# Attention with a mixture step: a new order of the first 12 blocks with K turned ahead of x, and a new end

## The chip, the cores and the metric

The kernel runs on one core of one Trainium2 chip. The core has five engines that run side by side: TensorE (matrix products; PE in the profile, its weight loads PEld), VectorE (DVE), ScalarE (ACT), GpSimd (POOL) and SyncE (SP), which here only issues DMAs. Each engine carries out its own list of instructions strictly in order and waits on semaphores for the others. The metric is the time of one execution on the device in microseconds (us), the median of several runs; lower is better.

## What is computed

The reference, cut to what matters (B=1, S=2048, D=640; 32 heads of width 192, a window of the last 512 keys):

```python
xn = layernorm(x)
q  = (xn @ wq).reshape(heads)                 # 2048 x 32 x 192
p  = softmax(q @ k[-512:].T * 192 ** -0.5)    # per head, 2048 x 512
s  = concat_heads(p @ v[-512:]) @ wo          # 2048 x 640
B  = xn, with an FFN result added to the 2 rows that score highest
out = x + s * silu(B)
```

All inputs and the output are bf16; sums are kept in fp32.

## The kernel before

The 32 heads are 8 groups of 4 (`GROUP`), a group is two head pairs, and the 2048 rows are 4 tiles of 512. A **step** is one group, one tile of 512 rows and one head pair (64 steps); it makes q for its pair, transposed, in three column sets c = 0, 1, 2 (`qT`, written by `q_whole` or the two-phase `q_phase`). A step is two **blocks** of 256 rows, 128 blocks in all, and a block has two halves a = 0, 1 of 128 rows. For a block b and half a:

- `S.b.a` (`scores`, line 367): six products of q and K into one of two score buffers in PSUM (`ps_s`, two buffers), 128 rows by 2 heads by 512 keys.
- `M.b.a` (`row_max`, line 372): VectorE takes the negated row maxima.
- `E.b.a` (`exps`, line 377): ScalarE takes the exponentials, one operation per head, and thereby empties the score buffer. Behind them SP issues a DMA that transposes the result into `pT`: one per half where b stands in `SPLIT`, otherwise one for the whole block.
- `P.b` (`o_item`): 32 products with V (line 406, `o_ps`), whose extra column is the row sum; VectorE takes its reciprocal, and VectorE (`v`) or ScalarE (`a`) scales each head's half into `o_sb`; SP issues the DMA that transposes it into `oT`.
- `W.k` (`w_item`, line 447): 24 products of `oT` with wo for two tiles of 128 rows and one half of the 640 output columns. In the first group they are copied into `s_acc`; in later groups they are added to it; in the last group each is multiplied by the gate, which lies in `xn` by then (line 473), and added to `s_acc`, which holds `s*g + x` by then (line 475 or 478), and stored (476, 479).

In the main loop (line 952) every block has the same fixed order (`BLOCK`). The head, blocks 0 to 11, and the end, blocks 126 and 127, follow two lists written out by hand, `FIRST` (line 602) and `LAST` (line 998). `first` and `last` turn each token into instructions; an engine gets its instructions in the order of the tokens. So the lists set, for each engine and for SP's DMA queue, who stands behind whom.

In the head the kernel also loads x, K, V, wq and wo; normalizes x (`st`, `nw`, `ap`, or `sa` for statistics on ScalarE; GpSimd takes some of the scalings, `ap.n.g`); transposes each normalized row tile on TensorE (`turn.n`, line 282, copied out by ScalarE or VectorE, line 283); turns the first K the same way (`kturn`, line 276) and later ones by DMA after a reordering on GpSimd (`ko`, `kT`); and doubles wo on GpSimd into the other 64 partitions (`wd`, line 151). q, P and W results and the turned tiles share four PSUM banks in turn (`f_tile`) until line 949, where they become one pair for q and two single banks for P and W.

In the end P of block 126 and 127 can't wait for DMA transposes, so the exponentials of block 127 (`U`, line 389) and the results of 126 and 127 (`T`, line 433) are turned on TensorE. W.124 to W.127 store each half of the columns by itself; the sums of W.124 and W.125 are GpSimd's, those of W.126 and W.127 VectorE's.

## Time and profile before

| | |
|---|---|
| median of 3 runs | 792.52 us (791.92 to 792.92) |
| profiled execution, its own time | 793.03 us |
| its span, first to last instruction | 791.3 us |
| TensorE busy | 777.6 us (98%) |
| VectorE, ScalarE, GpSimd busy | 579.0, 527.9, 338.8 us |
| mean granted TensorE clock | 0.998 |

The profile is of one execution. A row of the timeline gives the start in us from the span's beginning, the duration, the engine, the line of the kernel, the operation, what it writes and reads, and how many were merged; in square brackets stands how long the engine was idle before it and who ended that. A row of the groups gives the busy time of all of a kind, the mean of one in ns, and the idle time before them. The ends of matrix products are modelled, and one may overlap the next by about a tenth of a microsecond.

### The profile page before, as it was taken

How to read it: one execution, taken by the hardware profiler on the slowest of the kernel's cores; microseconds unless marked ns; L12 is line 12 of the kernel's file. 1: busy time of each engine (PE TensorE's matmuls, PEld its weight loads, DVE VectorE, ACT ScalarE, POOL GpSimd, SP SyncE). 2: the span in 40 equal slices, each digit the busy share in tenths (PEclk: the TensorE clock that was granted, in tenths of full speed). 3: DMA queues.
4: the chain of work that ended last, by engine and by line, in shares of the span. 5: the costliest groups of instructions: out<-in, count | busy, mean ns of one | idle time of the engine just before them, and what ended most of it. 6: DMA issues, size and time to landing. Idle time of an engine off the chain costs nothing.

```text
span 791.3 us, 26980 instructions
## 1 busy us (share of the span) xinstructions
PE 777.6 (98%) x11356; PEld 571.5 (72%) x11356; DVE 579.0 (73%) x1069; ACT 527.9 (67%) x954; POOL 338.8 (43%) x280
## 2 busy tenths in 40 slices
PE   8899999999999999999999999999999999999997
PEld 4457677777777777777777777777777777777775
DVE  7898788877777776767776766766766766776775
ACT  5676666667666677767666666766666666666662
POOL 1334110023110226626120101569977795256895
PEclk9999999999999999999999999999999999999999
DMA  9989999899999999999999999999999999999992
GB/s 231 199 175 170 175 190 167 141 189 164 174 193 186 179 200 199 184 174 195 179 195 198 190 206 191 159 190 188 159 171 185 148 180 183 185 171 167 187 186 84
DMA packets 447130, 142.18 MB, mean 180 GB/s; under 512 B 414180, under 2 KB 446438, under 8 KB 447008
## 3 DMA queue, kind: packets, MB, share of 16 engines
q1 hardware_dynamic: 437312, 130.88, 99.7%
q10 hardware_dynamic: 8672, 6.72, 3.3%
q0 software_dynamic: 1024, 2.85, 1.3%
q8 instruction: 89, 1.46, 0.8%
q14 instruction: 33, 0.27, 0.1%
HBM read 40.31 MB, written 2.63 MB: 54 GB/s over the span
## 4 chain that ended last, share of the span: by engine, by line
PE 89%; DMA 4%; DVE 3%; ACT 2%; issue 1%; SPq 0%; DVEq 0%; ACTq 0%
PE w L447 24%; PE q_ps L340 23%; PE o_ps L406 20%; PE s L367 19%; DMA oT<-o_sb 2%; DVE nm L372 2%; ACT pexp L377 1%; PE q_ps L309 1%; DMA x_in<-in_A_x_dram 1%; DMA pT<-pexp 1%; DMA v_sb<-in_A_v_cache_dram 1%; DMA xsT<-xsel 0%; DVE fin_o L475 0%; PE tp L282 0%; PE gu_ps L787 0%
## 5 line engine op out<-in xcount | busy, mean ns | idle before, releaser
L372 DVE TENSOR_REDUCE nm<-s 128x2 f32<-128x1024 f32 x256 | 312.9, 1223 | 137.8 <-PE s L367 136.1
L377 ACT ACTIVATE pexp<-s,nm 128x512 bf16<-128x512 f32 x512 | 324.1, 688 | 95.3 <-DVE nm L372 91.0
L340 PE MATMUL q_ps<-xnT,wq_g 64*128 64x512 bf16 (+1 forms) x2340 | 232.4, 323 | 0.0
L447 PE MATMUL w<-wo_g,oT 64*128 64x320 bf16 x3072 | 231.5, 296 | 0.2
L367 PE MATMUL s<-kT,qT 64*128 64x512 bf16 x1536 | 211.4, 376 | 2.5 <-ACT pexp L377 1.7
L447 PEld LDWEIGHTS <-oT 64*128 64x128 bf16 x3072 | 169.1, 94 | 59.7 <-DMA oT<-o_sb 1.4
L406 PEld LDWEIGHTS <-pT 64*128 64x128 bf16 x4096 | 177.3, 94 | 31.4 <-issue 2.8
L406 PE MATMUL o_ps<-v_sb,pT 64*128 64x193 bf16 x4096 | 195.3, 243 | 2.9 <-DMA pT<-pexp 1.8
L420 ACT ACTIVATE o_sb<-o_ps,rl 128x192 bf16<-128x192 f32 x250 | 91.6, 418 | 133.6 <-DVE rl L413 128.3
L340 PEld LDWEIGHTS <-wq_g 64*128 64x128 bf16 x2340 | 125.5, 99 | 46.1 <-DVE qT L313 0.5
L151 POOL COPY wo_g<-wo_g 64x1920 bf16<-64x1920 bf16 x32 | 57.4, 1797 | 189.4 <-DMA wo_g<-in_A_wo_dram 188.5
L367 PEld LDWEIGHTS <-qT 64*128 64x128 bf16 x1536 | 84.5, 94 | 57.6 <-DVE qT L313 3.0
L470 DVE TENSOR_TENSOR s_acc<-s_acc,w 128x320 f32<-128x320 f32 x192 | 84.9, 484 | 31.8 <-PE w L447 31.7
L352 ACT ACTIVATE qT<-q_ps 128x1024 bf16<-128x1024 f32 x114 | 92.4, 811 | 7.4 <-PE q_ps L340 1.4
L417 DVE TENSOR_TENSOR o_sb<-o_ps,rl 128x384 bf16<-128x384 f32 x131 | 73.0, 557 | 4.5
L121 POOL COPY k_perm<-k_raw 128x768 bf16<-128x768 bf16 x30 | 24.2, 827 | 95.4 <-DMA k_raw<-in_A_k_cache_dram 68.7
L877 POOL TENSOR_SCALAR yh<-y_bc,oh 128x640 f32<-128x640 f32 x32 | 60.3, 1886 | 5.4 <-DMA y_bc<-y_d 2.6
L878 POOL TENSOR_TENSOR xn<-xn,yh 128x640 bf16<-128x640 bf16 x32 | 45.0, 1406 | 2.7
L864 POOL TENSOR_TENSOR tz<-tz,xn 128x640 f32<-128x640 f32 x16 | 22.4, 1400 | 54.2 <-ACT tz L863 54.2
L413 DVE RECIPROCAL rl<-o_ps 128x2 f32<-128x2 f32 x256 | 30.5, 160 | 12.2 <-PE o_ps L406 7.6
L937 POOL TENSOR_TENSOR s_acc<-s_acc,x_fin 128x640 f32<-128x640 f32 x16 | 22.4, 1400 | 11.0 <-DMA x_fin<-in_A_x_dram 10.1
L865 POOL TENSOR_TENSOR xn<-tz,xn 128x640 bf16<-128x640 f32 x16 | 22.4, 1398 | 1.3
(138 smaller groups left out, 275.9 us busy)
## 6 DMA issues: line engine op xcount, KB each, us to landing
wo_g<-in_A_wo_dram SPq DMA_DIRECT2D x32, 240.0 KB, 4.2
k_raw<-in_A_k_cache_dram SPq DMA_DIRECT2D x32, 192.0 KB, 3.3
v_sb<-in_A_v_cache_dram SPq DMA_DIRECT2D x32, 192.0 KB, 4.1
wq_g<-in_A_wq_dram SPq DMA_DIRECT2D x14, 288.0 KB, 3.7
pT<-pexp SPq DMA_TRANSPOSE x246, 4.2
wq_g<-in_A_wq_dram SPq DMA_DIRECT2D x14, 192.0 KB, 3.1
x_fin<-in_A_x_dram SPq DMA_DIRECT2D x16, 160.0 KB, 3.8
oT<-o_sb SPq DMA_TRANSPOSE x126, 3.6
```

Of the source, the lines that this page charges most:

```text
L151: nc.gpsimd.tensor_copy(out=grp[g][("wo", pr)][half(1), cs, :], in_=grp[g][("wo", pr)][half(0), cs, :])
L340: mm = nc.tensor.matmul(q_ps[k][:, 0:n] if type(q_ps) is list else q_ps[:, k, 0:n], lhsT=wq[half(r), dc, c:2 * Dh:3], rhs=xnT[half(r), tok ...
L352: nc.scalar.activation(out=out, in_=q_ps[:, :, 0:n], func=ACT.Copy, scale=scale)
L367: nc.tensor.matmul(s_of[b, a][:, r, :], lhsT=qT_of[i][half(r), c, u * P:(u + 1) * P], rhs=grp[g][("kT", pr)][half(r), :, c, :], start=(c = ...
L372: rm = nc.vector.tensor_reduce(out=nm_of[b, a], in_=s_of[b, a], axis=AX.X, op=ALU.max, negate=True)
L377: nc.scalar.activation(out=p_ring[:, b % 2, a, :, hh, :].rearrange("p (x j) e -> p x j e", x=2), in_=s_of[b, a][:, hh, :].rearrange("p (j ...
L406: nc.tensor.matmul(o_of[b][r][:, a, 0:Dh + 1], lhsT=pT_ring[half(r), b % RP, a, k, :], rhs=v_ring[half(r), (g * PAIRS + pr) % RV, k, 0:Dh ...
L417: nc.vector.tensor_tensor(out=o_sb, in0=src, in1=rl[:, r].unsqueeze(2).unsqueeze(3).to_broadcast([P, 2, 3, HK]), op=ALU.mult)
L420: nc.scalar.activation(out=o_sb[:, a], in_=src[:, a], func=ACT.Copy, scale=rl[:, r, a:a + 1])
L447: nc.tensor.matmul(w_ps[r][:, 0:HD], lhsT=oT_ring[half(r), bs[pr] % RT, c, :], rhs=grp[g][("wo", pr)][half(r), c, cs], start=(pr == 0 and ...
L470: nc.vector.tensor_tensor(out=acc, in0=acc, in1=src, op=ALU.add)
L877: nc.gpsimd.tensor_scalar(out=yh, in0=M["y_bc"][:, j, :], scalar1=M["oh"][:, n, j:j + 1], scalar2=None, op0=ALU.mult)
```

## The change

The loads that begin the kernel become tokens of `FIRST`, so they can be ordered too: x tile 1 and then both windows of K are issued by ScalarE, x tiles 0, 2, 3 and then wq by SP. K is turned before the x tiles, and the order of all other work of the first 12 blocks is new. Whether a block's exponentials are transposed by half or whole is said by its token (`.s`); blocks 4 and 8 join those done by half, no block leaves them. The new `w_last` makes the last four W: for each of the two row tiles, its letter says whether VectorE multiplies in place in PSUM and adds from there (`v`), or VectorE multiplies into SBUF and GpSimd adds (`p`), and two more letters say which queue stores it. W.124 is `vv`, W.125 and W.126 are `pp`, and W.127 is made in two halves of 160 columns, each `vp`. The order of `LAST` is new in part: both turns of block 127 stand ahead of P.126, P.125 and P.127 are scaled by VectorE alone, and W.122 takes a score buffer.

```diff
-    nc.sync.dma_start(out=x_in[0][:, 0, :], in_=x_v[:, 0, :])
-    nc.scalar.dma_start(out=x_in[0][:, 1, :], in_=x_v[:, 1, :])
...
-    for hh in range(2):
-        k_piece(0, 0, hh, nc.sync)
-    wq_piece(0, 0, 0, nc.scalar)
-    for n in (2, 3):
-        nc.sync.dma_start(out=x_in[0][:, n, :], in_=x_v[:, n, :])
...
-    SPLIT = (0, 1, 2, 3, *range(HEAD, NB - 1))
...
+        if a == 0 and split:
+            split_of.add(b)
+        if b in split_of:
             nc.sync.dma_start_transpose(out=pT_ring[:, b % RP, a], in_=p_ring[:, b % 2, a].rearrange("p k h e -> p (k h e)"))
...
+    def w_last(k, where, how, cols):
+        g, n, cs, _ = w_of(k)
+        w_ps = w_banks(where)
+        w_products(k, w_ps, cols)
+        cs = slice(cs.start + cols[0], cs.start + cols[1])
+        t, o = fin_tiles(n)
+        for u in range(2):
+            src = w_ps[u][:, 0:cols[1] - cols[0]]
+            to = src if how[u] == "v" else t[:, u, cs]
+            nc.vector.tensor_tensor(out=to, in0=src, in1=xn[:, n + u, cs], op=ALU.mult)
+            (nc.vector if how[u] == "v" else nc.gpsimd).tensor_tensor(out=o[u][:, cs], in0=to, in1=s_acc[:, n + u, cs], op=ALU.add)
+            queues[how[2 + u]].dma_start(out=out_v[:, n + u, cs], in_=o[u][:, cs])
...
-                if k >= NB - 4:
-                    (nc.vector if last else nc.gpsimd).tensor_tensor(out=o[u][:, cs], in0=t[:, u, cs], in1=s_acc[:, n + u, cs], op=ALU.add)
-                    (nc.scalar if last and u else nc.sync).dma_start(out=out_v[:, n + u, cs], in_=o[u][:, cs])
...
     FIRST = """
-    v.0 x.1.0 bn.0.0 bn.1.0 x.1.1 bn.1.1 dev.1 bn.0.1 app.1 dev.0 k.1.0 app.0 bn.2.0 turn.0.a bn.3.0 bn.3.1 turn.1.a v.1 kturn.av bn.2.1 wq.1 dev.3 q.0.2.0.a k.1.1 q.0.0.0.v dev.2 v.2 q.0.1.0.a
-    ko.1 app.2 app.3 st.1.0
-    S.0.0 M.0.0 exp x.2 turn.2.a turn.3.a S.0.1 kT.1 M.0.1 st.1.1 E.0.0 st.1.2 wo.0 q.0.1.1.a q.0.0.1.a q.0.2.1.v E.0.1
-    S.1.0 wo.1 st.1.3 st.1.4 S.1.1 M.1.0 st.1.5 E.1.0 q.1.1.a M.1.1 q.1.2.a E.1.1 st.1.6 q.1.0.v st.1.7 nw.1.0
-    S.2.0 nw.1.1 nw.1.2 M.2.0 wo.2 S.2.1 nw.1.3 nw.1.4 nw.1.5 M.2.1 nw.1.6 st.2.0 E.2.0 ap.7.g ap.6.v P.0.vv E.2.1
-    S.3.0 M.3.0 ap.4.a v.3 S.3.1 turn.6.a ap.5.g wd.0 turn.5.a turn.4.v turn.7.v E.3.0 st.2.1 st.2.2 P.1.va M.3.1 wo.3 st.2.3 E.3.1 q.2.1.a q.2.2.v st.2.4 wd.1 q.2.0.v P.2.va
...
+    lx.1.a lx.0.s lx.2.s bn.1.0 lx.3.s bn.1.1 lq.0.s lk.0.a lk.1.a bn.0.0 dev.1 v.0 bn.0.1 x.1.0 bn.2.0 dev.0 app.0 app.1 bn.3.0 bn.2.1 kturn.av turn.0.a k.1.0 turn.1.a v.1 k.1.1 q.0.0.0.a dev.2 wq.1 bn.3.1 q.0.1.0.v x.1.1 app.2 v.2 st.1.0 q.0.2.0.a ko.1
+    S.0.0 dev.3 exp turn.2.a app.3 kT.1 turn.3.v M.0.0 x.2 E.0.0.s S.0.1 q.0.2.1.a q.0.0.1.a st.1.1 M.0.1 st.1.2 q.0.1.1.a q.1.0.a E.0.1 st.1.3
+    S.1.0 q.1.2.a S.1.1 wo.0 st.1.4 M.1.0 st.1.5 E.1.0.s q.1.1.a M.1.1 st.1.6 wo.1 E.1.1
+    S.2.0 wo.2 st.1.7 nw.1.0 nw.1.1 nw.1.2 M.2.0 nw.1.3 nw.1.4 S.2.1 M.2.1 v.3 wd.0 nw.1.5 nw.1.6 st.2.0 ap.5.g ap.7.v E.2.0.s E.2.1 ap.6.v P.0.va
+    S.3.0 st.2.1 ap.4.g wo.3 turn.7.a turn.6.a st.2.2 S.3.1 M.3.0 turn.5.a turn.4.a M.3.1 P.1.va q.2.0.a E.3.0.s q.2.2.v st.2.3 st.2.4 q.2.1.v E.3.1 wd.1 P.2.va
+    S.4.0 S.4.1 x.3 M.4.0 E.4.0.s M.4.1 st.2.5 st.2.6 st.2.7 E.4.1 wd.2 q.3.1.a nw.2.0 q.3.2.a nw.2.1
+    S.5.0 M.5.0 E.5.0 nw.2.2 q.3.0.v S.5.1 wd.3 M.5.1 sa.3.0.0 nw.2.3 E.5.1 nw.2.4 nw.2.5 sa.3.0.1 W.0.v nw.2.6 ap.8.g
+    S.6.0 ap.11.g sa.3.2.0 ap.9.g gk.0 W.1.a M.6.0 S.6.1 M.6.1 E.6.0 P.3.vv E.6.1 P.4.va st.3.6 turn.11.v ap.10.g gk.1
...
     LAST = """
-    S.126.0 M.126.0 W.120.q E.126.0 S.126.1 M.126.1 E.126.1 P.124.va B.126
-    S.127.0 M.127.0 W.121.q E.127.0 S.127.1 M.127.1 P.125.va E.127.1 W.122.q U.127.0.sa
-    O.126.vao U.127.1.sa W.123.s T.126.v O.127.vao W.124.s T.127.a W.125.s W.126.s W.127.q B.127
+    B.126 S.126.0 M.126.0 E.126.0 W.120.q S.126.1 M.126.1 E.126.1 P.124.vao S.127.0 M.127.0 W.121.q E.127.0
+    B.127 S.127.1 M.127.1 P.125.vvo W.122.s E.127.1 U.127.0.qv U.127.1.sa P.126.avo W.123.s T.126.a P.127.vvo W.124.s.vvss T.127.a W.125.o.ppss W.126.s.ppaa W.127.0.160.s.vpss W.127.160.320.q.vpsa
```

## The prediction

> **What bounds the kernel now.** First the page's engine shares, then a view of the busy time in three stretches (column 2 its length, column 3 TensorE).

> ```profile
> PE 777.6 (98%) x11356; PEld 571.5 (72%) x11356; DVE 579.0 (73%) x1069; ACT 527.9 (67%) x954; POOL 338.8 (43%) x280
> ...
> 75.00:760.00 685.00, 684.48 (x10212) 512.01 (x10210) 496.20 (x889) 465.54 (x832) 293.71 (x218) 1.00 1.08 181
> 7.00:75.00 68.00, 62.45 (x738) 39.04 (x740) 59.31 (x126) 48.03 (x96) 23.26 (x37) 1.00 0.98 191
> ```

> From 75 to 760 TensorE idles 0.52 us of 685, at full clock, and the edit touches nothing there. It can gain in two places: the 5.55 us that TensorE idles between 7 and 75, and the end. The matmuls are the same before and after. So I look for where TensorE waits in the new order. TensorE's own timeline of the head (start, duration, name, count, idle before it and who ended that):

> ```profile
> 1.19 5.73 PE L163 MATMUL warm_ps<-idle 128*128 128x512 bf16 x13 [1.19 <-DVE idle L160]
> ...
> 7.58 0.83 PE L276 MATMUL tp_k<-ident,k_raw 128*128 128x128 bf16 x12
> 8.81 1.80 PE L309 MATMUL q_ps<-xnT,wq_g 128*128 128x256 bf16 x15 [0.41 <-ACT xnT L283]
> 11.21 0.92 PE L367 MATMUL s<-kT,qT 64*128 64x512 bf16 x6 [0.60 <-ACT rstd L260]
> ...
> 21.97 1.47 PE L367 MATMUL s<-kT,qT 64*128 64x512 bf16 x12 [0.79 <-ACT pexp L377]
> ...
> 25.31 0.84 PE L406 MATMUL o_ps<-v_sb,pT 64*128 64x193 bf16 x16 [1.21 <-DMA pT<-pexp]
> ...
> 29.94 1.49 PE L406 MATMUL o_ps<-v_sb,pT 64*128 64x193 bf16 x31 [0.56 <-DVE xnT L283]
> 31.36 3.42 PE L309 MATMUL q_ps<-xnT,wq_g 128*128 128x512 bf16 x15
> ...
> 35.45 1.50 PE L406 MATMUL o_ps<-v_sb,pT 64*128 64x193 bf16 x31 [0.48 <-DMA v_sb<-in_A_v_cache_dram]
> ...
> 38.17 2.34 PE L309 MATMUL q_ps<-xnT,wq_g 128*128 128x512 bf16 x10
> ...
> 53.22 0.82 PE L367 MATMUL s<-kT,qT 64*128 64x512 bf16 x6 [0.44 <-ACT pexp L377]
> 53.97 3.42 PE L309 MATMUL q_ps<-xnT,wq_g 128*128 128x512 bf16 x15
> ```

> The head's operations by group (busy us, then mean ns of one), single rows of the timeline, and loads:

> ```profile
> L377 ACT ACTIVATE pexp<-s,nm 128x512 bf16<-128x512 f32 x46 | 29.1, 688 | 12.8 <-DVE nm L372 9.5 <-PE o_ps L406 3.2
> L372 DVE TENSOR_REDUCE nm<-s 128x2 f32<-128x1024 f32 x24 | 28.9, 1212 | 2.0 <-PE s L367 0.9 <-ACT pexp L377 0.5 <-ACT nw_a L232 0.4
> L283 ACT COPY xnT<-tp 128x640 bf16<-128x640 bf16 x7 | 4.6, 697 | 1.8 <-PE tp L282 1.8
> L315 ACT ACTIVATE qT<-q_ps 128x512 bf16<-128x512 f32 x6 | 3.5, 602 | 1.5 <-PE q_ps L309 1.5
> L277 ACT COPY kT<-tp_k 128x768 bf16<-128x768 bf16 x1 | 0.8, 817 | 0.0
> L511 ACT ACTIVATE xn<-x_in,sums 128x640 bf16<-128x640 bf16 x3 | 2.5, 841 | 0.0
> L466 ACT COPY s_acc<-w 128x320 f32<-128x320 f32 x2 | 0.8, 429 | 0.2 <-PE w L447 0.2
> ...
> 12.74 2.34 DVE L372 TENSOR_REDUCE nm<-s 128x2 f32<-128x1024 f32 x2
> ...
> 42.16 1.78 POOL L151 COPY wo_g<-wo_g 64x1920 bf16<-64x1920 bf16 x1
> ...
> 42.72 1.23 DVE L241 SCALAR_TENSOR_TENSOR nw_a<-rstd 128x4 f32<-128x4 f32 x1
> ...
> wq_g<-in_A_wq_dram ACTq DMA_DIRECT2D x1, 480.0 KB, 5.4
> k_raw<-in_A_k_cache_dram SPq DMA_DIRECT2D x2, 192.0 KB, 5.6
> ...
> 26.19 0.83 DVE L193 TENSOR_SCALAR xn<-x_in,rstd,nmr 128x640 bf16<-128x640 bf16 x1
> ...
> x_in<-in_A_x_dram SPq DMA_DIRECT2D x2, 640.0 KB, 6.0
> wo_g<-in_A_wo_dram SPq DMA_DIRECT2D x5, 240.0 KB, 3.8
> ...
> pT<-pexp SPq DMA_TRANSPOSE x14, 4.3
> ...
> x_in<-in_A_x_dram SPq DMA_DIRECT2D x1, 640.0 KB, 5.0
> ```

> The last fence's final rows are DMA issues (KB each, median us from issue to landing); of the two 640 KB loads one took 5.0, so the other about 7.0.

> **Part 1, K ahead of x.** K's two windows leave SP's queue for ScalarE's, behind x tile 1, the second issued about 1.9. By the 5.6 of its row it lands by 7.5, but 320 KB of x stand ahead of it in place of the 480 KB of wq: I take 7.0 (never below 6.92, where the warm-up matmuls end, 1.19+5.73). wq now stands fourth on SP, issued about 2.1; by its row 7.5, and with K's bytes beside it under 9, while q asks for it at 9.65: no wait. On SP the next load of K waits, as before, until its slot is free; K is turned at 7.85 rather than 8.41 (7.58+0.83), so the loads behind it start 0.5 earlier, and the second part of x tile group 1 goes behind wq.1 instead of ahead of K: nothing asks for it before 18.

> K's turn then ends at 7.83, ScalarE copies half of K (0.82, from 7.5) and two x tiles (1.29 as a pair), so q starts at 9.65, 0.85 later than at 8.81. Before, K's copies came behind and held q's evictions; now these follow at once, and the first scores start at 11.45 against 11.21. **+0.25.**

> **Part 2, to the first P products.** VectorE now has tile 3's scaling and its copy ahead of the first maximum, and that scaling waits for a ScalarE step behind q's last eviction (ends 12.15). Scaling to 13.0, five transposes and the copy 0.95: maximum at 13.95, not 12.74; its exps begin at 15.2. From there ScalarE has no pause: four pairs of exps (4x1.27; two of 0.688 overlap a little), three whole q evictions (3x0.60) and three of half size (estimated 3x0.33) end at 23.1, and scores 2.1 waits for that buffer, ending at 23.8 (before 23.4, 21.97+1.47). But P of block 0 runs through: its last transpose is issued at 19.4 and lands by 23.7, so the 1.21 us wait goes, and P ends at 25.2 against 26.0 or so (25.31+0.84, less the overlap of the next). **Here 0.8 ahead.**

> **Part 3, block 3.** GpSimd's doubling of wo (1.78) now stands ahead of its two scalings. wo is issued at 20.75, lands 3.8 later, so the doubling runs 24.5 to 26.25. VectorE's last Newton steps are due at 25.5. The pair of rows 42.16 and 42.72 shows what such a step does then: 1.23 us for four columns, and it ends when GpSimd's copy ends (42.16+1.78). So the scalings start at 26.6, VectorE's own (behind a statistic, alternating with GpSimd's) end at 27.8 and 28.8. TensorE, done with scores 3.0 at 25.9, waits some 1.9 us for tile 7 and 0.6 for tile 6. Then four copies on ScalarE (4x0.65), behind P's eviction, let q start at 32.4 (before 31.36). The v wait (0.48) goes: v.3 is issued before the transposes now. q of step 3 starts at 38.55 against 38.17. **+0.4: the lead is lost.**

> **Part 4, to block 12.** SP issues x.3 behind the transpose of P.2's result, at 39.9, and it lands by its row's kind at 45. ScalarE sums a row of it (priced as its neighbour L511, about 0.9) ahead of exps 5.1 (1.27), which end at 47.2, as TensorE ends W.1 (47.4): hidden, but without slack. W.1's copies (0.8 for both, on ScalarE) stand behind two squarings (0.84, with what reads their sums about 1.0 each) and end at 49.8, where P.4 wants its bank at 49.3: +0.5; the 0.44 wait before 53.22 goes. Scores 9.1 wait about 0.2 more than their like before. **+0.2.** Two more transposes of half size for blocks 4 and 8 cost SP an issue each beside TensorE's work, nothing. Sum of the head: 0.4+0.2 = **+0.6**, bounds -1.2 (no locked step, no wait at P.4) and +2.6 (x.3 late, below).

> [...]

> **Part 5, the end.** The timeline of the last 22 us:

> ```profile
> 769.79 0.84 PE L406 MATMUL o_ps<-v_sb,pT 64*128 64x193 bf16 x16 [0.61 <-DMA pT<-pexp]
> ...
> 780.42 5.06 PE L447 MATMUL w<-wo_g,oT 64*128 64x320 bf16 x72
> ...
> 781.41 0.56 POOL L479 DMA_DIRECT2D out_dram<-fin_o  x1 [0.30 <-POOL fin_o L478]
> 781.99 3.32 POOL L475 TENSOR_TENSOR fin_o<-fin_t,s_acc 128x320 bf16<-128x320 f32 x4
> ...
> 784.50 1.18 DVE L475 TENSOR_TENSOR fin_o<-fin_t,s_acc 128x320 bf16<-128x320 f32 x1
> 785.60 0.48 DVE L473 TENSOR_TENSOR fin_t<-w,xn 128x320 f32<-128x320 f32 x1
> ...
> 786.68 2.17 ACTq L476 DMA_DIRECT2D out_dram<-fin_o  x2
> ...
> 787.96 0.49 DVE L475 TENSOR_TENSOR fin_o<-fin_t,s_acc 128x320 bf16<-128x320 f32 x1
> ```

> TensorE ends at 785.5, VectorE's last sum at 788.45, since one sum took 1.18 beside GpSimd's and eight operations of 0.48 queue for the last two W. The last store's issue ends at 788.85 (786.68+2.17) and the span 2.45 us later; that tail stays. The first 0.61 us wait, for block 125's transpose, stays too: nothing ahead of it changes.

> New: W.124's sums on VectorE read PSUM (4x0.48, 780.0 to 782.0); products of 125 and 126 by 783.1 and 784.75; their sums on GpSimd (0.83 to 0.88 each, 3.32 for four), the last of them also behind the landing of an earlier store from its buffer (row 781.41), until 786.2. Both halves of P.125 and P.127 on VectorE, both turns of 127 ahead of P.126 and W.122 in a score buffer make TensorE wait for nothing: by these durations each buffer is empty 0.3 us or more before it is asked for. If that cover went, T.127 would be late first, behind P.127's second eviction. Block 127 in halves of 160 columns: 24 matmuls at best 0.82 (half of 1.63), at worst 1.0 (the 193-column product takes 0.84 for 16, that is 0.042 each in a row of them); I take 0.95 and lose 0.25. VectorE's half operations lie between 0.24 and 0.48; 0.32. First half at 784.7 to 785.7, second at 785.7 to 786.65; GpSimd's two half sums (0.44 to 0.88, I take 0.6) end at 787.4. Last store 787.45, not 788.5: **-1.05**. Bounds: -1.5 (short sums), -0.3 (full-size prices for the halves).

> Sum: +0.6-1.05 = -0.45. The profiled execution took 793.03 with a span of 791.3; the median of the runs is 792.52. **792.1.**

> **Rivals.** *Faster:* part 3's locks don't bite, since wo lands after the Newton steps or VectorE slips between two GpSimd operations (a scaling in this trace did). Turn 7 starts at 26.8, q at 31.3, and P.4 finds its bank: head -1.1, end -1.1: 790.3. It decides from a turn 7 at about 27.2. Against it: 3.8 us for wo is a median of five.

> *Slower:* x.3. ScalarE's sum of it stands ahead of exps 5.1, and scores 6.1 now follow W.1 directly, where P.3 lay between. Its 5.0 to 7.0 us (the 6.0 is the mean of two) put TensorE's wait at 0 to 1.9; at 8, 2.8: 792.1+2.8 = 794.9. It decides from about 7 us on; against it, the transposes before it are few.

> [...]

> **How the numbers follow.** Changes under 0.2% (1.6 us) count as none; that is about what a measurement of this kernel can tell. Forecast, 792.1: 0.36; K late: 0.08; faster: 0.30; x.3 and other waits behind ScalarE: 0.26. So faster 0.30, same 0.44, slower 0.26. The range runs from the faster rival's far bound, 789.9, to the slower one's price, 794.9; the forecast's own is 791.0 to 793.6.

> **What would show it.** Right: first scores near 11.45, the first maximum at 13.95, no DMA wait at P of block 0, a gap of about 2 us before tile 7's turn with a Newton step of over 0.5 us, q of step 4 near 54.5 (now 53.97), the last store near 787.5 plus 0.6. Wrong: a gap under 1 us there (faster), or TensorE idle before scores 6.1 with ScalarE waiting for x_in (slower).

## The result and the profile after

The changed kernel takes 794.6 us (median of 16 runs, 793.25 to 797.49), the kernel before 792.43 on the same chip (16 runs, 790.92 to 795.38). The ratio is 1.0027, interval 1.0017 to 1.0037: slower by 0.27%, where I forecast 792.1 and no change. The profiled execution took 794.58 with a span of 792.8 (before 793.03 and 791.3).

TensorE's timeline of the changed kernel's head (start, duration, name, count, idle before it and who ended that):

```profile
8.19 0.83 PE L268 MATMUL tp_k<-ident,k_raw 128*128 128x128 bf16 x12 [1.44 <-DMA k_raw<-in_A_k_cache_dram]
8.86 0.72 PE L274 MATMUL tp<-ident,xn 128*128 128x128 bf16 x10
10.77 1.80 PE L300 MATMUL q_ps<-xnT,wq_g 128*128 128x256 bf16 x15 [1.19 <-ACT xnT L275]
12.49 0.93 PE L358 MATMUL s<-kT,qT 64*128 64x512 bf16 x6
...
14.87 0.45 PE L274 MATMUL tp<-ident,xn 128*128 128x128 bf16 x5 [1.06 <-DVE xn L256]
...
25.39 1.51 PE L401 MATMUL o_ps<-v_sb,pT 64*128 64x193 bf16 x32
26.89 0.82 PE L358 MATMUL s<-kT,qT 64*128 64x512 bf16 x6
29.24 0.45 PE L274 MATMUL tp<-ident,xn 128*128 128x128 bf16 x5 [1.53 <-DVE xn L185]
30.16 0.58 PE L274 MATMUL tp<-ident,xn 128*128 128x128 bf16 x5 [0.47 <-DVE xn L185]
30.67 1.46 PE L358 MATMUL s<-kT,qT 64*128 64x512 bf16 x6
32.07 1.25 PE L274 MATMUL tp<-ident,xn 128*128 128x128 bf16 x10
33.25 1.74 PE L401 MATMUL o_ps<-v_sb,pT 64*128 64x193 bf16 x32
34.92 3.42 PE L300 MATMUL q_ps<-xnT,wq_g 128*128 128x512 bf16 x15
...
56.04 3.42 PE L300 MATMUL q_ps<-xnT,wq_g 128*128 128x512 bf16 x15
```

Three things are to be seen. K's turn starts at 8.19, since K is not there (1.44 of waiting for its DMA). Tiles 3 and 7 are waited for, 1.06 and 1.53. And the rows from 30.67 on are too long for what they do: six score products take 1.46 where the row at 26.89 has 0.82, and ten transposes 1.25 where the row at 8.86 has 0.72. q of step 4 starts at 56.04, 2.07 later than before (53.97).

The granted clock explains the long rows. Busy time by stretches of half a microsecond, same kernel (the eighth number from the left, behind the five engines, is the clock):

```profile
29.00:30.00 1.00, 0.45 (x5) 0.28 (x5) 1.00 (x2) 0.00 (x0) 0.94 (x3) 1.00 1.26 188
30.00:30.50 0.50, 0.34 (x5) 0.31 (x5) 0.47 (x4) 0.29 (x1) 0.50 (x1) 0.85 1.37 187
30.50:31.00 0.50, 0.50 (x5) 0.13 (x4) 0.50 (x2) 0.50 (x3) 0.50 (x1) 0.50 1.89 116
...
33.50:34.00 0.50, 0.50 (x14) 0.48 (x12) 0.50 (x1) 0.50 (x2) 0.00 (x0) 0.74 0.07 16
```

From about 30.35 to 33.75 TensorE ran at half its clock, right after 2.0 us of idle time out of 2.45 (27.71 to 30.16). In the profile of before the clock is 1.00 from block 0 up to 788.6, when TensorE has long finished.

VectorE and GpSimd, same kernel, from the timeline of all engines:

```profile
7.21 0.45 DVE L256 TENSOR_SCALAR xn<-x_in,mv,rstd 128x640 bf16<-128x640 bf16 x1
...
13.76 1.05 DVE L256 TENSOR_SCALAR xn<-x_in,mv,rstd 128x640 bf16<-128x640 bf16 x1
13.81 0.82 POOL L119 COPY k_perm<-k_raw 128x768 bf16<-128x768 bf16 x1 [0.74 <-DMA k_raw<-in_A_k_cache_dram]
...
25.98 1.78 POOL L149 COPY wo_g<-wo_g 64x1920 bf16<-64x1920 bf16 x1 [1.62 <-DMA wo_g<-in_A_wo_dram]
26.93 0.85 DVE L239 SCALAR_TENSOR_TENSOR rstd<-nw_a,rstd 128x4 f32<-128x4 f32 x1
...
90.78 1.78 POOL L149 COPY wo_g<-wo_g 64x1920 bf16<-64x1920 bf16 x1 [2.84 <-DMA wo_g<-in_A_wo_dram]
91.13 2.11 DVE L686 SCALAR_TENSOR_TENSOR junk<-xn,wr_bc 128x640 bf16<-128x640 bf16 x1
...
100.39 0.81 DVE L686 SCALAR_TENSOR_TENSOR junk<-xn,wr_bc 128x640 bf16<-128x640 bf16 x1
```

Three VectorE operations lie beside a GpSimd copy and take longer than by themselves: the scaling of tile 3 1.05 (tile 1's, at 7.21, 0.45), the Newton step of four columns 0.85 (it ends with the copy, 25.98+1.78), and a product in block 13 2.11 (0.81 one block later). In each of the three GpSimd's copy runs its usual 0.82 or 1.78. Behind the last one TensorE waits 0.77 ahead of W at 95.27.

The end, same kernel:

```profile
783.06 5.09 PE L443 MATMUL w<-wo_g,oT 64*128 64x320 bf16 x96
783.90 6.26 SPq L469 DMA_DIRECT2D out_dram<-fin_o  x7
785.48 4.33 POOL L468 TENSOR_TENSOR fin_o<-fin_t,s_acc 128x320 bf16<-128x320 f32 x6 [0.88 <-DVE fin_t L467]
787.41 0.32 DVE L467 TENSOR_TENSOR w<-w,xn 128x160 f32<-128x160 f32 x1
788.07 2.12 ACTq L469 DMA_DIRECT2D out_dram<-fin_o  x3
```

TensorE ends at 788.15 (783.06+5.09), and the last store's issue at 790.19 (788.07+2.12), 2.0 us later; before it was 3.36 (785.49 to 788.85). From the second half of P of block 125 to the end of the span it is 20.2 us (772.63 to 792.8), before 21.5 (769.79 to 791.3). So the span's +1.5 is: head +2.07, the stretch between head and end +0.8 (the wait at 95.27 is nearly all of it), end -1.3.

### The profile page after: what moved, and what is told of

It is laid out like the page before. It is cut to its first block, busy times and chain, and to the rows that moved or that the text cites. A ratio compares the mean times of both kernels' runs of the same rounds, so it can differ in the third digit from the quotient of the medians.

```text
span 792.8 us, 27049 instructions
## 1 busy us (share of the span) xinstructions
PE 778.3 (98%) x11380; PEld 574.2 (72%) x11380; DVE 576.0 (73%) x1059; ACT 530.3 (67%) x963; POOL 340.9 (43%) x284
## 3 DMA queue, kind: packets, MB, share of 16 engines
q8 instruction: 89, 1.46, 0.8%
## 4 chain that ended last, share of the span: by engine, by line
PE 92%; DVE 2%; ACT 2%; DMA 2%; POOL 1%; issue 1%; ACTq 0%; POOLq 0%; DVEq 0%
PE w L443 25%; PE q_ps L331 24%; PE o_ps L401 20%; PE s L358 20%; PE q_ps L300 2%; DMA k_raw<-in_A_k_cache_dram 1%; DMA pT<-pexp 1%; PE tp L274 1%; DVE nm L363 1%; ACT pexp L370 1%; ACT o_sb L415 0%; POOL fin_o L468 0%; POOL fin_o L487 0%; DVE junk L686 0%; PE gu_ps L799 0%
## 5 line engine op out<-in xcount | busy, mean ns | idle before, releaser
L443 PE MATMUL w<-wo_g,oT 64*128 64x320 bf16 (+1 forms) x3096 | 231.4, 295 | 0.8 <-ACT o_sb L415 0.8
L443 PEld LDWEIGHTS <-oT 64*128 64x128 bf16 x3096 | 171.1, 94 | 58.7 <-issue 1.3
L408 DVE RECIPROCAL rl<-o_ps 128x2 f32<-128x2 f32 x256 | 30.6, 160 | 15.5 <-PE o_ps L401 10.9
## 6 DMA issues: line engine op xcount, KB each, us to landing
v_sb<-in_A_v_cache_dram SPq DMA_DIRECT2D x32, 192.0 KB, 4.0
k_raw<-in_A_k_cache_dram SPq DMA_DIRECT2D x30, 192.0 KB, 3.1
wq_g<-in_A_wq_dram SPq DMA_DIRECT2D x14, 192.0 KB, 3.2
```

What stands on the lines that cost most here:

```text
L443: nc.tensor.matmul(w_ps[r][:, 0:cs.stop - cs.start], lhsT=oT_ring[half(r), bs[pr] % RT, c, :], rhs=grp[g][("wo", pr)][half(r), c, cs], sta ...
```

## The experiments

The theories. *Late K*: K, on ScalarE's queue and sharing the DMA engines with x (between 3 and 4 us SP's packets took 56.7% of the 16 engines' time and ScalarE's 49.9%), lands later than on SP's queue ahead of x tiles 2 and 3 (8.06 here, 7.44 in the profile of before, 6.8 to 7.0 in the six profiles below that turn K first and load as before). *Lock*: GpSimd's copy ahead of its scalings holds VectorE, and so tile 7. *Clock*: the idle time that follows costs a second time, by a lower clock. Rivals: the loss lies in the rest of the new order, or in the new end. All kernels compute the whole output; where TensorE does extra work, its expectation says so.

Results first, by kind. "Clock" is the lowest mean granted clock among a kernel's executions, "tile 7" the idle time ahead of that turn, "K's turn" its start and "q4" the start of q of step 4, these three in the profiled execution:

| kernel | ratio to before | clock | K's turn | tile 7 | q4 |
|---|---|---|---|---|---|
| changed | 1.0027 (1.0017 to 1.0037) | 0.992 | 8.19 | 1.53 | 56.04 |
| changed, again | 1.0038 (1.0023 to 1.0053) | 0.992 | 7.71 | 2.43 | 55.99 |
| old head, new end | 0.9987 (0.9972 to 1.0002) | 0.998 | after x | | 53.99 |
| new head, old end | 1.0039 (1.0021 to 1.0057) | 0.992 | 7.40 | 1.91 | 53.47 |
| old loads | 1.0001 (0.9991 to 1.0012) | 0.996 | 7.05 | 2.43 | 56.24 |
| wq behind K | 1.0016 (0.9997 to 1.0035) | 0.993 | 7.82 | 1.63 | 53.80 |
| copy behind | 0.9996 (0.9984 to 1.0009) | 0.994 | 7.78 | 0.78 | 53.65 |
| tile 7 filled | 1.0016 (1.0002 to 1.0030) | 0.994 | 8.36 | 0.29 | 56.33 |
| gaps filled | 1.0016 (1.0002 to 1.0030) | 0.998 | 8.96 | 0.43 | 56.80 |
| old loads, copy behind | 0.9998 (0.9985 to 1.0012) | 0.996 | 6.93 | 0.78 | 54.04 |
| mended head, new end | 0.9964 (0.9951 to 0.9977) | 0.998 | 6.99 | 0.77 | 51.94 |
| the same, no fill | 0.9961 (0.9946 to 0.9976) | 0.998 | 7.12 | 0.78 | 52.08 |
| mended head, old end | 0.9978 (0.9968 to 0.9988) | 0.998 | 6.91 | 0.77 | 51.40 |
| K second on each queue | 0.9976 (0.9964 to 0.9988) | 0.998 | 7.47 | 0.78 | 54.47 |

All executions of the kernel before beside them have clocks of 0.996 or above. One stretch of 3.4 us at half the clock lowers the mean of a span of 791 us by 0.002. The mean also counts the end of the span: in the profile of before the clock is 0.50 from 788.6 on, after TensorE's last product (785.49), and the mean is 0.998. So 0.998 does not exclude one stretch in the head, and 0.995 or less takes more than one.

**Head and end apart.** Both kernels are put together from the two lists:

```diff
 # old head, new end: FIRST of before (with its loads ahead of it), LAST as changed
 # new head, old end: FIRST as changed, LAST and last sums of before
```

> The head as before (order and loads), the end as in the changed kernel. If the head alone lost (its scores, q and P products start 2.1 us later at block 12: 87.79 against 85.70) and the end gained as I forecast, this is 0.8 to 1.1 us below the kernel before: 791.4 to 791.6, last product and last store the same distance apart as in the changed kernel. If the end also lost or gave nothing, it is within 0.3 us of the kernel before, 792.4.

> The head as in the changed kernel, the end as before. If the two parts simply add, this is the kernel before plus 2.1 for the head, plus up to 1.1 more than the changed kernel: 794.5 to 795.5, block 12 at 86.7 as in the changed kernel. If the end is what lost, it is near 792.4.

The old head with the new end: 791.85 against 793.41, ratio 0.9987, interval up to 1.0002. That is the size I forecast, though the interval just takes in 1. From P of block 125 to the end its span has 20.4. The new head with the old end: 795.88, ratio 1.0039, end 21.6 (770.82 to 792.4). So the loss is the head's and the end gains. But its profiled execution has an earlier q of step 4 than before, 53.47. TensorE's timeline of that execution:

```profile
25.27 0.82 PE L359 MATMUL s<-kT,qT 64*128 64x512 bf16 x6
28.00 0.45 PE L274 MATMUL tp<-ident,xn 128*128 128x128 bf16 x5 [1.91 <-DVE xn L185]
28.92 0.45 PE L274 MATMUL tp<-ident,xn 128*128 128x128 bf16 x5 [0.47 <-DVE xn L185]
29.30 0.82 PE L359 MATMUL s<-kT,qT 64*128 64x512 bf16 x6
30.06 0.73 PE L274 MATMUL tp<-ident,xn 128*128 128x128 bf16 x10
```

The same waits as in the changed kernel, the first even longer, and yet the scores behind them take 0.82 and the transposes 0.73: here the clock did not fall. Whether it falls differs between executions of one head; the last section sets these two side by side. What this execution won by block 12 it lost behind it, by waits of 1.02 (W in block 13), 0.36 and 0.17.

**K's loads put back.**

```diff
-    lx.1.a lx.0.s lx.2.s bn.1.0 lx.3.s bn.1.1 lq.0.s lk.0.a lk.1.a
+    lx.0.s lx.1.a lk.0.s lk.1.s lq.0.a lx.2.s lx.3.s bn.1.0 bn.1.1
```

> The changed kernel with one thing put back: the order and queues of the first loads (x tiles 0, 2, 3 and both K windows on SP, K ahead of x tiles 2 and 3; x tile 1 and wq on ScalarE's queue). K is still turned ahead of x. Theory late K: K lands at 7.4 instead of 8.06, K's turn starts at 7.5 instead of 8.19 and all of the head comes 0.6 to 0.8 earlier: 793.9, q of step 4 at 55.3. Theory order: the loss sits in what follows the first scores (tile 3 ahead of the first maximum, GpSimd's copy ahead of its scalings), the earlier K only makes the gaps there longer: 794.6, gap ahead of tile 7's turn over 2 us.

K's turn starts at 7.05 and the first scores at 12.05, 0.44 earlier than in the changed kernel. Then the timeline of all engines:

```profile
26.14 1.78 POOL L149 COPY wo_g<-wo_g 64x1920 bf16<-64x1920 bf16 x1 [2.52 <-DMA wo_g<-in_A_wo_dram]
26.18 1.75 DVE L239 SCALAR_TENSOR_TENSOR rstd<-nw_a,rstd 128x4 f32<-128x4 f32 x1
...
29.40 0.45 PE L274 MATMUL tp<-ident,xn 128*128 128x128 bf16 x5 [2.43 <-DVE xn L185]
```

The Newton step took 1.75, up to the end of the copy, the gap grew from 1.53 to 2.43, and the clock fell to 0.50 (31.0 to 34.4): q of step 4 at 56.24. In this trace the lock takes all that the earlier K gave, which the expectation called theory order. Over its eleven executions, though, the time is that of before, 0.26% below the changed kernel's ratio, and none has a clock under 0.996.

**The copy behind the scalings.**

```diff
-    ... v.3 wd.0 nw.1.5 nw.1.6 ... ap.4.g wo.3 turn.7.a
+    ... v.3 nw.1.5 nw.1.6 ... ap.4.g wd.0 wo.3 turn.7.a
```

> The changed kernel with one GpSimd operation moved: the first doubling of wo (1.78 us) stands behind the scalings of tiles 5 and 4 instead of ahead of them. Theory lock: the Newton step of 0.85 that ends with the doubling takes 0.16, GpSimd's scaling no longer waits behind the doubling, tile 7's turn starts 0.7 to 1.0 earlier than 29.24 and the gaps of 1.53 and 0.46 shrink to some 1.0 together: 793.6 to 793.9. Theory late K alone: the gap there is set by the late first maximum (two exps and maxima late), not by the doubling: under 0.2 us, 794.6.

```profile
26.62 0.15 DVE L239 SCALAR_TENSOR_TENSOR rstd<-nw_a,rstd 128x4 f32<-128x4 f32 x1
...
28.18 0.45 PE L274 MATMUL tp<-ident,xn 128*128 128x128 bf16 x5 [0.78 <-DVE xn L185]
...
28.92 1.78 POOL L149 COPY wo_g<-wo_g 64x1920 bf16<-64x1920 bf16 x1
```

The Newton step is 0.15 again, the gaps 0.78 and 0.47 (1.25 against 2.0), as the theory lock said. The clock stays at 1.00, and q of step 4 comes at 53.65, 2.4 earlier than in the changed kernel: 0.4 from an earlier K in this execution, 0.75 from the gaps, some 1.2 from the clock. The ratio, 0.9996, is 0.3% below the changed kernel's.

**wq behind K.**

```diff
-    lq.0.s lk.0.a lk.1.a
+    lk.0.a lk.1.a lq.0.a
```

> The changed kernel with one load moved: wq of the first head pair goes behind K's two windows on ScalarE's queue, instead of ahead of the later SP loads. Theory late K: wq's 480 KB no longer share the DMA engines with K's 384, K lands at about 7.2 in every execution and the first scores come at about 11.6; 0.8 below the changed kernel (-0.1%), the more so as TensorE idles less. If x's bytes and not wq's held K back: K at 8.0 as before, no change. If wq now comes late (landing above 10), TensorE waits for it ahead of q: up to 1 us lost.

K's turn still waits 1.33 for the DMA and starts at 7.82: wq is not what holds K back. The expected 7.2 and 11.6 for the first scores failed (12.12). The ratio, 1.0016, is unclear beside 1.0027. Its executions fall into two sets: six with a clock of 0.999 or 1.000 have a median of 792.1, the time of the kernel before (792.17), and six of 0.997 or less one of 795.0. Since a later K lengthens TensorE's waits and its idle time at once, this does not separate the price of the clock from that of the waits.

**TensorE kept busy in the gaps.** Extra transposes of a zero tile, or products of zeros, into the bank that the next real operation overwrites:

```diff
+        for _ in range(fills.pop("n", 0)):
+            nc.tensor.transpose(out=tp[:, 0, :], in_=idle[:, 0:P], identity=ident)
-    ... turn.7.a turn.6.a
+    ... fill.18 turn.7.a fill.4 turn.6.a
```

> The changed kernel with 18 extra transposes of a zero tile ahead of tile 7's turn and 4 ahead of tile 6's, into the bank that the turn writes anyway: TensorE works where it idled 1.53 and 0.46 us, the waits for VectorE stay as they are. Theory clock: the granted clock stays at 1.00 between 30 and 34 (0.50 from 30.5 to 33.6 in the changed kernel), scores 3.1, two turns and P.1 take 0.82, 0.73 and 1.5 instead of 1.46, 1.25 and 1.74, and q of step 2 starts 1.2 to 1.4 earlier with tile 7's turn where it was: 793.2 to 793.8 (-0.15%). Theory waits alone: no gain, or 0.1 to 0.3 lost to the extra work.

> The changed kernel with extra work for TensorE in each long gap of the head: 17 instead of 13 warm-up matmuls, 8 zero products ahead of the first q, 12 zero transposes ahead of tile 3's turn, 18 and 4 ahead of tiles 7 and 6. No wait is taken away. Theory clock: the clock of every execution is 0.998 or above (0.992 to 1.000 in those of the changed kernel), the spread narrows, and the median is 1.5 to 2 below the changed kernel: 792.6 to 793.1. Theory waits alone: the same as the changed kernel, or up to 0.5 slower because K's turn may come behind the longer warm-up.

With tile 7 alone filled the clock stays at 1.00 from 28 to 34 (scores 0.82, two turns 0.73), as the theory clock said there. But in this execution K's turn came at 8.36 after 2.46 us of idle time, and the clock fell earlier, for 6.8 us (8.15 to 14.98). Busy time by stretches:

```profile
6.00:8.00 2.00, 0.00 (x0) 0.00 (x0) 1.92 (x8) 0.29 (x1) 0.00 (x0) 1.00 1.12 300
8.00:10.00 2.00, 1.64 (x16) 1.68 (x17) 0.79 (x4) 0.80 (x1) 0.00 (x0) 0.54 1.07 175
10.00:12.00 2.00, 1.16 (x11) 0.94 (x9) 1.00 (x3) 1.29 (x2) 0.00 (x0) 0.50 0.67 180
```

The first q took 3.36 here, not 1.80. So there are two places where the clock falls, the wait for K and tile 7. With all long gaps filled, none of 12 executions has a clock below 0.998, where 14 of the changed kernel's 27 lie below 0.996. That is the clearest evidence that the idle time brings the clock down. The expected 792.6 to 793.1 did not come: 793.82, ratio 1.0016, whose interval overlaps that of the changed kernel, so a gain in time is not shown. In its profile K is the latest of all (turn at 8.96), though the longer warm-up ended at 6.97, and a further wait stands in place of the lost one, TensorE's 1.30 ahead of scores 6.1. ScalarE's timeline there:

```profile
44.52 1.27 ACT L375 ACTIVATE pexp<-s,nm 128x512 bf16<-128x512 f32 x2 [0.18 <-DVE nm L368]
48.24 0.74 ACT L521 ACTIVATE xn<-x_in 128x640 bf16<-128x640 bf16 x1 [2.46 <-DMA x_in<-in_A_x_dram]
```

That is the prediction's slower rival, x.3 late ahead of exps 5.1. It landed 5.7 us after its issue (42.54 to 48.22); in the changed kernel's own profile it was issued at 42.09, landed at 47.04, and nobody waited. My "from about 7 us on" counted from an issue at 39.9, and the issue came over 2 us later; the rival is real.

**Both put back.**

```diff
 # loads as in "K's loads put back", wd.0 as in "the copy behind the scalings"
```

> The changed kernel with both put back: the first loads in the old order and queues, and the doubling of wo behind the scalings of tiles 5 and 4. If late K, the lock and the clock drop that follows it are the whole loss, the head is 0.5 to 1.0 earlier than in the kernel before at q of step 4 (53.0 to 53.5 against 53.97) and the new end's gain of 0.8 to 1.0 comes through: 790.6 to 791.2, faster than both. If a loss is left in the order of the head, 791.8 to 792.4.

792.26 against 792.17: only the loss is gone, and the hoped-for 790.6 to 791.2 missed. In the profile q of step 4 comes at 54.04, and the clock fell once more, from 10.2 to 13.6 (q in 3.36). That alone does not explain the miss: the six executions with a clock of 0.999 or 1.000 have a median of 791.9. The idle time before the fall, 0.60 and 0.82, comes from tile 1: VectorE has the statistics of tile 2 ahead of the scalings of tiles 0 and 1, and with the old loads tile 2 lands at 7.2.

**The first maximum ahead of tile 3,** on the same base:

```diff
-    S.0.0 dev.3 exp turn.2.a app.3 kT.1 turn.3.v M.0.0
+    S.0.0 M.0.0 dev.3 exp turn.2.a app.3 kT.1 turn.3.v
```

> Old loads and the doubling behind the scalings, and the first row maximum put ahead of tile 3's scaling and copy on VectorE. If the new place of the maximum cost 1.2 as I forecast: the first maximum starts as the first scores end instead of some 2 us later, tile 3's turn waits up to 1.2 longer, exps 0.0 start 1.5 to 2 earlier, and scores 2.1 and P of block 0 come 0.5 to 1 earlier after the first scores than in the kernel without the move (first scores to P of block 0: 12.9 us in the changed kernel). If the late tile 3 costs as much: no change there.

A single execution took 791.7. The first maximum starts at 13.07, as the first scores end, exps 0.0 at 14.67 (17.02 in the changed kernel), tile 3 is waited for 1.49. P of block 0 starts 13.2 us after the first scores, no sooner than the changed kernel's 12.9. In this one execution the order of the two gains nothing: TensorE waits longer for tile 3, so scores 0.1 start 3.2 us after the first scores (2.8 in the changed kernel), and the earlier exps do not help what stands behind them.

**The head mended,** with what these runs taught:

```diff
-    ... bn.2.0 dev.0 app.0 app.1 bn.3.0 bn.2.1 kturn.av turn.0.a k.1.0 turn.1.a v.1 k.1.1 q.0.0.0.a
+    ... dev.0 app.0 app.1 bn.2.0 kturn.av turn.0.a k.1.0 turn.1.v v.1 k.1.1 fill.4 q.0.0.0.a bn.3.0 bn.2.1
 # and the loads and wd.0 as above
```

> A candidate built on the two edits put back together: first loads in the old order, doubling of wo behind the scalings; and in the first 10 us VectorE scales tiles 0 and 1 ahead of the statistics of tile 2 (whose landing at 7.2 held both), VectorE instead of ScalarE copies tile 1's turn, and four zero products run ahead of the first q. Theory (late K, the lock and the clock are all that the new head loses): q starts at 9.1 instead of 10.8, first scores near 10.8, q of step 4 near 53, clock 0.998 or above in all executions, and with the new end's 1.2 the time is 790.2 to 791.0, 0.2% below the kernel before. Rival (the order after the first scores costs what an early start gains): 792.

789.42 against 792.58: ratio 0.9964, interval 0.9951 to 0.9977, faster than both kernels. TensorE's timeline:

```profile
6.99 0.83 PE L269 MATMUL tp_k<-ident,k_raw 128*128 128x128 bf16 x12 [0.99 <-DMA k_raw<-in_A_k_cache_dram]
...
9.07 1.80 PE L305 MATMUL q_ps<-xnT,wq_g 128*128 128x256 bf16 x15 [0.26 <-DVE xnT L278]
10.80 0.93 PE L363 MATMUL s<-kT,qT 64*128 64x512 bf16 x6
...
26.02 0.45 PE L277 MATMUL tp<-ident,xn 128*128 128x128 bf16 x5 [0.77 <-DVE xn L185]
...
51.94 3.42 PE L305 MATMUL q_ps<-xnT,wq_g 128*128 128x512 bf16 x15
```

q and first scores come where they were expected, 9.07 and 10.80, and q of step 4 is 2.0 earlier than before; I had expected 53.

**One window of K on each queue,** on the mended head:

```diff
-    lk.0.s lk.1.s
+    lk.0.s lk.1.a
```

> The same with one of K's two windows on each queue, second behind one x tile, ahead of wq and of x tiles 2 and 3. Theory that K's landing is set by the bytes that the queues bring ahead of it and beside it: both windows land by 6.0 (6.8 to 7.4 in the old order, 7.3 to 8.8 in the changed kernel), wq at about 7.5, x tile 3 still near 8. If the landing hangs on the 384-byte packets themselves: 6.8 or later. In time the same as the kernel beside it within 0.5 us, since TensorE's warm-up ends at 6.9 in any case.

The expectation for K failed in the profile. The window on ScalarE's queue landed at 4.67, but the one on SP's at 7.34, and wq, third on ScalarE's queue, only at 10.53:

```profile
8.14 0.72 PE L277 MATMUL tp<-ident,xn 128*128 128x128 bf16 x10
...
10.57 1.82 PE L305 MATMUL q_ps<-xnT,wq_g 128*128 128x256 bf16 x15 [1.27 <-DMA wq_g<-in_A_wq_dram]
```

So in this execution a load's landing is not given by the bytes that stand ahead of it on its queue; how the two queues share the DMA engines stays open. The median is 790.86, ratio 0.9976, but the profiled execution took 794.38, the longest of the eight, so its late wq need not be typical.

**The last block whole,** on the old head with the new end:

```diff
-    W.127.0.160.s.vpss W.127.160.320.q.vpsa
+    W.127.s.vpsa
```

> The old head with the new end, but block 127's W whole: no halves. From the first product of block 125 to the end of the span the kernel before takes 21.5 (769.79 to 791.3), the changed one 20.2. If the halves pay (last sums and store half as long against 0.25 more of products): 20.5 to 20.9 here. If the gain comes from the sums' place alone: 20.2 or less.

A single execution took 791.97, and 20.6 us from P of block 125 to the end (769.30 to 789.9). With halves it was 20.2 to 20.7 in twelve profiles, mostly 20.2. TensorE needs the same 15.5 either way, so the halves cost nothing measurable; whether they gain can't be told from it.

**The changed kernel beside the mended one, and its parts.**

> The changed kernel itself, beside the other two on one chip. Theory (late K, lock, clock drop together): over the kernel before by 0.2 to 0.35%, some executions with a clock of 0.992 to 0.996, none of the next two below 0.997.

> The mended head (old loads, tiles 0 and 1 scaled first, VectorE copies tile 1, the doubling behind the scalings) with the new end, without the four zero products ahead of q. If the clock falls only where TensorE idles long, the 0.26 and 0.6 us gaps that are left keep it up: the same as with the zero products, 0.3 to 0.4% below the kernel before, clock 0.998 or above. If the fill carries part of the gain: clocks of 0.996 to 0.997 in some executions and 1 us more.

> The mended head with the four zero products and the old end. If head and end add: the new end's 1.2 us are missing, 0.15% above the same head with the new end (0.9964), 0.9975 to 0.9985 of the kernel before; from the first product of block 125 to the end of the span 21.5 instead of 20.2 to 20.4.

The changed kernel again: 795.0 against 792.42, ratio 1.0038, and again a locked Newton step (1.75), a gap of 2.43 and half the clock behind it. Taken over its 27 executions in two sets, those with a clock of 0.996 or more have medians of 793.95 and 794.3, those below it 795.35 and 796.8: so the lower clock goes with 1.4 to 2.5 us more in half of the executions. It is not the whole loss: the four executions with a clock of 0.998 or more took 792.97 to 794.23, with a median 1.4 above the kernel before. The mended head without the zero products: 0.9961, the same as with them, so they are not what pays. The mended head with the old end: 0.9978, so of the gain of some 2.9 us about 1.75 is the head's and 1.1 to 1.3 the end's, and the end's share agrees with the traces (21.6 against 20.5 and 20.7).

## Why the prediction was wrong

The step that failed is part 1's "I take 7.0" for K's landing, which came at 8.06, and with it a term that the sum lacked altogether: what TensorE's idle time does to its own clock, 1.3 us in the profile. K's own row had given 7.5; I took off 0.5 by the bytes ahead of it on its queue, and no run supports that way of reckoning. That 794.6 lies inside my range is luck: its upper end, 794.9, was the price of a late x.3, which cost nothing in this profile.

- **Part 1.** K landed at 8.06, not 7.0, so the turn ended at 9.0 instead of 7.83. What I built on it held: q 1.75 after the turn's end (1.82 taken), the first scores 1.7 after that (1.8). To a late K I had given 0.08. In six more profiles with K on ScalarE's queue its turn starts at 7.40 to 8.96; in the six with both windows on SP's queue at 6.91 to 7.12, where the warm-up has hardly ended. That K comes later on ScalarE's queue is shown; the reason is not. Between 3 and 4 us the trace has 171 packets of SP's queue and 315 of ScalarE's. That wq holds it back is not confirmed: with wq behind it, K still landed at 7.68.
- **Part 2.** First maximum 15.77, 3.3 after the first scores where I had 2.5. Of this 0.8, 0.6 is the scaling of tile 3, 1.05 instead of 0.45, beside GpSimd's reordering of K. I had looked for the lock in block 3 alone. P of block 0 ran without its DMA wait, as forecast, but ended at 26.9, not 25.2.
- **Part 3.** The lock was right: a Newton step of 0.85 (1.75 in two other profiles) that ends with the copy, and gaps of 1.53 and 0.47 (1.9 and 0.6 taken). The two experiments that move or keep the copy show it. The step took 1.75 beside the copy in "old loads" and 0.15 ahead of it in "copy behind". But I counted the gap only as its length. The half clock behind it cost 1.3 more: from tile 7's turn to q of step 2 it is 5.68 here and 4.35 in "new head, old end" and in "copy behind", where the clock stayed. In other executions it came at K's wait too. With the 1.04 from the first scores that is nearly all of the 2.5 by which q of step 2 (34.92) missed my 32.4.
- **Part 4.** Too dark by about 1 us: from q of step 2 to q of step 4 it took 21.1 instead of my 22.1, because the wait for P.4's bank (0.5) did not come, nor any other between the two. x.3 was issued at 42.09, not 39.9; it landed in time in this profile, and late in another. That the wait stayed away here is luck.
- **Part 5.** Right: -1.3 against -1.05, inside its bounds. Two halves took 1.82 (2 x 0.95 taken), the whole before 1.80, so the 0.25 that I had set against them did not come; the 160-column operations took 0.32 as taken.
- **Between head and end** I had set nothing. The 0.8 there is another lock, in block 13, where the new order brings wo's doubling beside a VectorE product (90.78 and 91.13; 93.36 and 89.04 before). It comes and goes between executions: "copy behind" has the same code there and no such wait. There the product began first (88.73, the copy 89.18), took its 0.81, and the copy took 2.01 instead of 1.78.

So the sum of the trace is +2.07 +0.8 -1.3 against my +0.6 -1.05, and the medians, with the clock falling more than once in half of the executions, are +2.2. The end came as forecast; the forecast of no change was wrong by the new head and by what it leaves behind in block 13.

## What to carry to other kernels

Price an idle stretch of TensorE not only by its length but by the clock behind it: here two gaps of 2 us together cost 1.3 us more, and not in every execution. When a first load is moved to another queue, look at its landing in several executions: here K's turn started at 7.40 to 8.96 with the loads on ScalarE's queue and at 6.91 to 7.12 with them on SP's, and an order that hangs on the moved load waits for the late ones too. When GpSimd gets a long copy, check which VectorE operations will lie beside it; here moving the copy behind its scalings cost nothing (0.9996 against 1.0027) and took the lock away (a Newton step of 0.15 against 0.85 to 1.75).

## What the runs showed of the hardware

```profile
26.94:30.35 3.41, 1.42 (x15) 0.65 (x15) 3.34 (x9) 1.40 (x3) 2.96 (x4) 1.00 1.26 223
30.35:33.76 3.41, 3.41 (x29) 1.87 (x28) 3.38 (x6) 2.71 (x6) 3.15 (x2) 0.50 1.15 198
...
24.06:27.48 3.42, 2.03 (x36) 1.27 (x30) 3.36 (x6) 2.42 (x4) 2.35 (x2) 1.00 1.36 212
27.48:30.89 3.41, 2.42 (x27) 1.43 (x28) 3.34 (x9) 1.92 (x5) 3.35 (x4) 1.00 1.10 180
```

The changed kernel's gaps of 1.53 and 0.47 lie within one step, TensorE was busy 1.42 of it (0.42), and the next step ran at half the clock. In the other execution the longer gaps of 1.91 and 0.47 are shared out between two steps, each was busy for 0.59 or more, and the clock stayed. Ahead of four of the five falls seen in a head the share was 0.15 to 0.42; ahead of the fifth ("old loads, copy behind", 6.81 to 10.22) it was 0.55. Shares of 0.49 (the changed kernel, 6.46 to 9.87) and 0.48 ("copy behind", 6.56 to 9.97) let the clock stay. So the bound, and what counts as busy, are not shown.

No idle stretch of TensorE as long as one such step lies ahead of the five falls in a head: the longest was 2.46 us in "tile 7 filled", 1.53 in the changed kernel, and 0.82 with "old loads, copy behind".

A VectorE scaling with one bf16 input in SBUF, 0.45 by itself, took 1.05 beside a GpSimd copy of 0.82; the Newton step and the product of block 13, which have two inputs, took 0.85 and 2.11 beside copies of 1.78 (0.15 and 0.81 by themselves). In block 13 VectorE's product took 2.11 where the copy began 0.35 ahead of it, and the copy 2.01 where the product began 0.45 ahead. At tile 3 the scaling began 0.05 ahead of the copy (13.76 and 13.81), and still it was the scaling that took longer, while the copy took its usual 0.82.
